# Unit 10's transpose moved from DMA to TensorE, and the unit loads two ahead from unit 10 on

## Chip, cores, metric

One core of one Trainium2 chip; the experiments ran on three chips, and each is compared with before on its own chip. The metric is the device time of one execution in microseconds (us). Times are medians, with the lowest and highest in brackets. The profiled span runs from the first to the last instruction and is about 1.7 us shorter than the time of the same run.

## The reference, cut

```python
# attention with decay: q, k, v (4, 8, 768, 64) float32, lam (8,), blocks along the sequence
intra = (q_b @ k_b.T) * Dmask;  intra = intra @ v_b
inter = (q_b * lam_pow) @ kv_state
out_b = intra + inter
kv_state = lam_block * kv_state + (k_b * rev_pow).T @ v_b
# then x = out, (3072, 512):   a = x @ w_a;  b = x @ w_b;  y = (a * b) @ w_out    # d_ff 1536
```

## The kernel before, the parts that matter

The work is cut into 24 units of 128 tokens, in feed-forward groups of 4, 1, 2, 4, 4, 4, 4 and 1 units. While TensorE does the feed-forward matmuls of one group, the attention pieces of later units are slipped in at numbered slots. In group 2, slots 0 to 11 follow the `a` and `b` matmuls of f = 0 to 11 (the twelve slices of 128 columns of d_ff), and slots 12 to 15 the half rows of the output matmuls `op`. `P` prepares a unit (scaling of k and q on GpSimd, cast of v, and the next loads), `T` transposes on TensorE, `S` makes scores and masks, `V` updates the state, `Q` and `O2` do inter, (scores,) intra. Units 0 to 8 are transposed on TensorE, units 9 to 23 by a DMA transpose that SP issues.

```python
LOOKAHEAD = (3, 2)
DMA_T_FROM = 9
PLAN = { ...
    2: [(0, "V", 6), (1, "T", 7), (1, "P", 8), (4, "T", 8), (4, "P", 9), (6, "S", 7),
        (6, "S", 8), (7, "V", 7), (6, "P", 10), (10, "V", 8),
        (12, "Q", (7, 8, 9, 10)), (12, "P", 11), (13, "V", 9), (14, "P", 12),
        (14, "O2", (9, 10))],
    3: [(3, "S", 11), (3, "S", 12)], ... }

def pump():                       # issue what may be issued, in order, on SP
    while pending:
        kind, c = pending[0]
        if kind in "abo": ...     # weights
        elif c >= used["u"] + LOOKAHEAD[used["u"] > 11]:
            return
        ...

def prep_k(u):
    make_ks(u, "dve" if u < n0 + 2 else "pool")
    make_qs(u, "pool")
    used["u"] = u + 1
    if u >= DMA_T_FROM:
        qkT = qkT_pool.tile(...)
        nc.sync.dma_start_transpose(out=qkT..., in_=U[u]["qk"]...)

def prep_v(u):
    make_vb(u, ...)
    pump()                        # the loads come after this unit's transpose

def piece_T(u):
    tps = ps_bank("tps", [128, 2, HP, 128], BF16)      # one of 7 rotating PSUM banks
    for j in range(2):
        for hp in range(HP):
            nc.tensor.transpose(tps[:, j, hp, :], d["qk"][:, j, 2*hp:2*hp+2, :], ident)
    qkT = qkT_pool.tile(...)
    nc.scalar.copy(qkT, tps)
```

## Time and profile before

| | before |
|---|---|
| time | 234.9 us (234.56 to 235.3) |
| profiled span (that run took 235.62 us) | 233.9 us |
| TensorE busy | 225.5 us, 96% of the span |
| DMA transposes / TensorE transposes `tps` | 15 / 40 |

The kernel is full of TensorE work, so the question is only where TensorE has a hole. The profile's first part, the group of the PSUM copies, and the line of the DMA transposes (count, median us from issue to landing):

```profile
PE 225.5 (96%) x1775; PEld 124.7 (53%) x1775; DVE 118.3 (51%) x204; ACT 91.1 (39%) x172; POOL 50.6 (22%) x65
...
L298 ACT COPY qkT<-tps 128x1024 bf16<-128x1024 bf16 x5 | 5.1, 1012 | 9.9 <-PE tps L296 9.9
```

```profile
qkT<-qk SPq DMA_TRANSPOSE x15, 4.2
```

### The profile page before, as it was taken

What the parts mean: (1) busy time and instruction counts of PE and PEld (TensorE: products, weight loads), DVE (VectorE), ACT (ScalarE), POOL (GpSimd) and SP (SyncE); (2) the same over time, 40 slices, a digit from 0 to 9 for tenths busy, and PEclk for the clock granted to TensorE, in tenths of its full rate; (3) what the DMA queues carried; (4) which work ended last, traced back from release to release, by engine and by line L of the source; (5) the groups of instructions that cost most, each with busy time, mean ns of one, the idle gap of its engine ahead of it and who ended that gap; (6) DMA issues with size and microseconds to landing.
All of it is one profiled execution on the core that took longest, in us unless ns stands there. A gap on an engine that the chain in (4) does not pass through costs nothing.

```text
span 233.9 us, 4520 instructions
## 1 busy us (share of the span) xinstructions
PE 225.5 (96%) x1775; PEld 124.7 (53%) x1775; DVE 118.3 (51%) x204; ACT 91.1 (39%) x172; POOL 50.6 (22%) x65
## 2 busy tenths in 40 slices
PE   7799999999999799999999999999999999999993
PEld 2474444459688454454544454544454544444493
DVE  0896557536579536775235574235583323332050
ACT  3585753066363243342243342333332333332261
POOL 6070000237463333553000543001200000000000
PEclk9999999999999999999999999999999999999999
DMA  4999999999999999998659997229300220000311
GB/s 154 301 286 350 349 366 288 295 191 224 198 229 174 207 220 203 213 193 162 234 198 215 211 178 134 90 90 207 67 3 0 90 92 0 1 0 23 114 45 48
DMA packets 96389, 38.84 MB, mean 166 GB/s; under 512 B 83312, under 2 KB 91888, under 8 KB 96368
## 3 DMA queue, kind: packets, MB, share of 16 engines
q1 hardware_dynamic: 96224, 38.54, 73.3%
q8 instruction: 14, 0.23, 0.4%
q14 instruction: 7, 0.06, 0.1%
q10 hardware_dynamic: 144, 0.00, 0.0%
HBM read 28.32 MB, written 6.29 MB: 148 GB/s over the span
## 4 chain that ended last, share of the span: by engine, by line
PE 90%; DMA 5%; ACT 1%; SPq 1%; issue 0%; DVE 0%
PE a_ps L435 27%; PE b_ps L435 26%; PE op L467 26%; DMA k<-in_k_dram 3%; PE o_ps L352 3%; PE kq L310 2%; DMA qkT<-qk 2%; PE o_ps L342 2%; PE kvd L366 1%; PE tps L296 1%; ACT o_kept L458 1%; SPq L209 1%; PE kq L578 1%; ACT xT L359 0%; PE kv L366 0%; PE tk L542 0%
## 5 line engine op out<-in xcount | busy, mean ns | idle before, releaser
L447 DVE TENSOR_TENSOR ab<-a_sb,b_ps 128x512 bf16<-128x512 bf16 (+2 forms) x96 | 52.5, 553 | 76.7 <-PE b_ps L435 56.7
L435 PE MATMUL a_ps<-xT,wa_sb 128*128 128x512 bf16 (+2 forms) x384 | 77.2, 326 | 0.6 <-ACT xT L359 0.6
L435 PE MATMUL b_ps<-xT,wb_sb 128*128 128x512 bf16 (+2 forms) x384 | 77.3, 326 | 0.0
L442 ACT CAST a_sb<-a_ps 128x512 bf16<-128x512 f32 (+2 forms) x96 | 45.6, 481 | 63.2 <-PE a_ps L435 61.6
L467 PE MATMUL op<-wo_sb,ab 128*128 128x512 bf16 (+2 forms) x312 | 65.6, 363 | 0.0
L435 PEld LDWEIGHTS <-wb_sb 128*128 128x128 bf16 x384 | 34.5, 98 | 28.6
L435 PEld LDWEIGHTS <-wa_sb 128*128 128x128 bf16 x384 | 33.7, 98 | 29.0 <-POOL wa_sb L162 0.6
L467 PEld LDWEIGHTS <-ab 128*128 128x128 bf16 x312 | 28.8, 98 | 29.9
L327 DVE TENSOR_TENSOR m<-kq,lotri 128x512 bf16<-128x512 f32 x47 | 29.4, 684 | 19.3 <-PE kq L310 19.0
L259 POOL TENSOR_TENSOR qk<-kf,lp_k 128x512 bf16<-128x512 f32 x18 | 19.0, 1057 | 76.4 <-DMA kf<-in_k_dram 69.8
L264 POOL TENSOR_TENSOR qk<-qf,lp_q 128x512 bf16<-128x512 f32 x20 | 21.7, 1087 | 23.4 <-DMA qf<-in_q_dram 23.4
L462 ACT COPY o_sb<-op 128x512 f32<-128x512 f32 (+2 forms) x19 | 10.3, 541 | 34.0 <-PE op L467 34.0
L359 ACT CAST xT<-o_ps 128x512 bf16<-128x512 f32 x22 | 12.0, 590 | 19.6 <-PE o_ps L352 19.2
L398 DVE TENSOR_TENSOR st<-kvd,bdiag 128x512 bf16<-128x512 f32 x18 | 12.3, 685 | 4.7 <-PE kvd L366 3.6
L273 DVE CAST vb<-vf 128x512 bf16<-128x512 f32 x17 | 11.3, 667 | 0.0
L298 ACT COPY qkT<-tps 128x1024 bf16<-128x1024 bf16 x5 | 5.1, 1012 | 9.9 <-PE tps L296 9.9
L197 PE MATMUL idle<-idle_sb 128*128 128x128 bf16 (+1 forms) x31 | 7.5, 384 | 1.3 <-DVE idle_sb L192 1.3
L310 PE MATMUL kq<-qkT 64*128 64x128 bf16 x160 | 6.7, 218 | 1.5 <-DMA qkT<-qk 1.5
L352 PE MATMUL o_ps<-m,vb 128*64 128x128 bf16 x192 | 7.9, 222 | 0.0
L273 POOL CAST vb<-vf 128x512 bf16<-128x512 f32 x7 | 4.7, 674 | 13.9 <-DMA vf<-in_v_dram 13.9
L342 PEld LDWEIGHTS <-st 128*128 128x128 bf16 x80 | 5.4, 98 | 2.8
L352 PEld LDWEIGHTS <-vb 128*64 128x64 bf16 x192 | 5.8, 109 | 1.4
(57 smaller groups left out, 87.4 us busy)
## 6 DMA issues: line engine op xcount, KB each, us to landing
vf<-in_v_dram SPq DMA_DIRECT2D x24, 256.0 KB, 5.1
qf<-in_q_dram SPq DMA_DIRECT2D x20, 256.0 KB, 4.5
kf<-in_k_dram SPq DMA_DIRECT2D x20, 256.0 KB, 4.8
out_dram<-o_sb SPq DMA_DIRECT2D x16, 256.0 KB, 2.0
wst<-in_moe_w_a_dram SPq DMA_DIRECT2D x6, 512.0 KB, 8.7
wst<-in_moe_w_b_dram SPq DMA_DIRECT2D x6, 512.0 KB, 8.8
wst<-in_moe_w_out_dram SPq DMA_DIRECT2D x6, 512.0 KB, 8.5
out_dram<-o_kept SPq DMA_DIRECT2D x7, 256.0 KB, 2.5
```

What stands on the lines that cost most here:

```text
L259: eng_of(eng).tensor_mul(qk[:, 1], raw.pop((u, "k")), lp_k[:, u % NB].to_broadcast([128, H, D]))
L264: eng_of(eng).tensor_mul(U[u]["qk"][:, 0], raw.pop((u, "q")), lp_q[:, u % NB].to_broadcast([128, H, D]))
L273: eng_of(eng).tensor_copy(vb, vf)
L310: nc.tensor.matmul(kq[i][:, hp, :], lhsT=d["kT"][p, hp, :], rhs=d["qT"][p, hp, :], start=True, stop=True, skip_group_check=True)
L327: nc.vector.tensor_mul(m, kq[i], lotri_bc)
L352: nc.tensor.matmul(d["o"][p, hp, :], lhsT=d["vb"][:, 2 * hp + i, :], rhs=d["m"](i, hp), start=(first and hp == 0), stop=True, skip_group_c ...
L359: nc.scalar.copy(xT[:, :, col:col + BLK], o_ps)
L398: nc.vector.tensor_mul(st[:].rearrange("p hp i d -> p hp (i d)"), ps[:].rearrange("p hp i d -> p hp (i d)"), bdiag_bc)
L435: nc.tensor.matmul(ps[:, :gt], lhsT=w_sb[:, s, f * 128:(f + 1) * 128], rhs=xT[:, s, :gt], start=(s == 0), stop=(s == KS - 1))
L442: nc.scalar.copy(a_sb[:, :gt], ps[:, :gt])
L447: nc.vector.tensor_mul(ab[:, f, :gt], a_sb[:, :gt], ps[:, :gt])
L467: nc.tensor.matmul(op[:, lo:hi], lhsT=ab[:, f, t * 128:(t + 1) * 128], rhs=wo_sb[:, f, lo:hi], start=(f == 0), stop=(f == FC - 1))
```

## The change

Intent: unit 10's transpose comes too late for its scores, so TensorE does it itself, and the loads are held back one unit from unit 10 on. Unit 9 stays with the DMA.

```diff
-        (6, "S", 8), (7, "V", 7), (6, "P", 10), (10, "V", 8),
+        (6, "S", 8), (7, "V", 7), (6, "P", 10), (9, "T", 10), (10, "V", 8),
-            elif c >= used["u"] + LOOKAHEAD[used["u"] > 11]:
+            elif c >= used["u"] + LOOKAHEAD[used["u"] > 9]:
-        if u >= DMA_T_FROM:
+        if u >= DMA_T_FROM and u != 10:
```

## The prediction

> **What bounds the kernel now.** I read four things in this order: who TensorE waited for, how full TensorE is before and after its longest wait, the instruction around that wait, and the queue that issued the transfer it waited for. All are of the kernel before; its profiled span is 233.9 us against a timed median of 234.9 us.
>
> The list of waits of TensorE (total us, times, longest us), whole for waits over 0.6 us:
>
> ```profile
> PE kq L310 <- DMA qkT<-qk: 1.5, 1, 1.5
> PE idle L197 <- DVE idle_sb L192: 1.3, 1, 1.3
> PE tk L542 <- DVE scratch L531: 0.7, 2, 0.3
> ```
>
> The second and third belong to the first 20 us (warm-up and the packed first group). The only wait of any size in the steady part is the first: the scores `kq` waited once, for a DMA transpose. Busy time of TensorE in stretches (window, length, busy, granted clock, DMA share, GB/s):
>
> ```profile
> 60.00:77.50 17.50, 17.50 (x191) 1.00 1.23 197
> 77.50:79.10 1.60, 0.11 (x6) 1.00 0.98 210
> 79.10:230.40 151.30, 151.24 (x1094) 1.00 0.57 120
> 230.40:233.90 3.50, 0.00 (x0) 1.00 0.22 65
> ```
>
> TensorE has no gap for 17.5 us ahead of that wait and none worth a name for the 151 us after it, at full clock. So the kernel is bound by TensorE, the end moves one for one with TensorE work from 60 us on, and all there is to win here is this one hole. The hole in TensorE's timeline (start, length):
>
> ```profile
> 76.62 0.61 PE L342 MATMUL o_ps<-qkT,st 128*128 128x128 bf16 x8
> 77.16 0.40 PE L310 MATMUL kq<-qkT 64*128 64x128 bf16 x8
> 79.05 0.40 PE L310 MATMUL kq<-qkT 64*128 64x128 bf16 x8 [1.49 <-DMA qkT<-qk]
> ```
>
> This is slot 12 of group 2, `Q (7, 8, 9, 10)`: inter of 7 and 8, scores of 9 (eight matmuls, no wait), scores of 10 (eight, after 1.49 us). So it is unit 10's transpose alone that is late. Why it is late stands in the issue queue of SP and on GpSimd, which makes its source:
>
> ```profile
> 68.12 1.04 POOL L264 TENSOR_TENSOR qk<-qf,lp_q 128x512 bf16<-128x512 f32 x1
> ```
>
> ```profile
> 68.06 2.21 SPq L282 DMA_TRANSPOSE qkT<-qk  x1
> 70.33 0.56 SPq L128 DMA_DIRECT2D qf<-in_q_dram  x1
> 70.94 1.66 SPq L128 DMA_DIRECT2D kf<-in_k_dram  x1
> 72.71 0.83 SPq L128 DMA_DIRECT2D vf<-in_v_dram  x1
> 74.12 1.86 SPq L282 DMA_TRANSPOSE qkT<-qk  x1
> 76.04 0.57 SPq L128 DMA_DIRECT2D qf<-in_q_dram  x1
> 76.67 1.07 SPq L128 DMA_DIRECT2D kf<-in_k_dram  x1
> 77.83 0.86 SPq L128 DMA_DIRECT2D vf<-in_v_dram  x1
> 78.81 3.70 SPq L282 DMA_TRANSPOSE qkT<-qk  x2
> ```
>
> I match these to units by counting: the nine GpSimd pairs up to 92 us are units 6 to 14, and by the program's order the transposes here are 9, 10, then 11 and 12 together, with the loads of unit 12 between 9 and 10 and those of unit 13 between 10 and 11. Unit 10's `qk` was ready at 68.12 + 1.04 = 69.16 us. Its transpose was issued at 74.12, five microseconds later, because SP issues in order and was busy with transpose 9 and the three loads of unit 12. The chain of work that ended last says the rest, and what a transpose on TensorE costs (start, length):
>
> ```profile
> 67.80 0.45 PE tps L296 x8
> ...
> 74.12 4.89 DMA qkT<-qk
> ```
>
> **What the Trainium skill says.** "Perfetto Trace Analysis", section "What "DMA-bound" means", names as a bound of its own the issuing sequencer whose track is solid with DMA slices, this being descriptor generation. The trace agrees for 54.5 to 90 us: SP's slices follow each other within about 0.6 us, a transpose taking 1.86 to 2.21 us. "Advanced Engine Details and Errata", section "X-Bar Transpose (TRN2)", has transposes as fast as ordinary DMAs at 350 to 400 GB/s, for 256 KB an estimated 0.7 us; in this trace they need 3.0 to 5.9 us from issue to landing (median 4.2), so I use the trace. "TensorE: Matmul & The Clock Gate", section "Part 4: PE-mode transpose", gives some 275 ns for one transpose in a kernel, into PSUM, with a copy after it. Here one shows 219 ns, but eight in a row push the next matmul back by only 0.45 us, and the copy on ScalarE takes 1012 ns. Last, "SBUF — State Buffer" says that VectorE and GpSimd share a port pair as an exclusive lock; the `vb` casts at 0.42 to 1.20 us in 60 to 90 us fit that, and I use it only for a margin below.
>
> **The change part by part.**
> 1. Removed: transpose 10 on SP (1.86 us of the queue) and its 4.89 us to landing. The hole of 1.49 us goes if nothing else is late.
> 2. Added on TensorE: eight transposes in slot 9 of group 2. Slot 9 follows the `b` matmuls of f = 9, which end at 73.33 us. The source was ready at 69.16, so there is no wait. Cost +0.45 us, in full on the path, as TensorE has no slack there.
> 3. Added on ScalarE: one copy of 1.01 us, from about 73.97 to 74.98 (0.19 us after the eight end, as for unit 8). It delays the copy `a_sb` of f = 10 from 73.97 to 74.98, f = 11 from 75.09 to about 75.35, then VectorE's product of f = 11 from 76.1 to about 76.8 at its end. That product first matters for the last six `op` matmuls of the row, at about 79 us, and as the release of the PSUM bank that inter of 8 takes. Counting the seven rotating banks through the new order (one more bank taken, by `tps`), unit 8's `o_ps` falls on the bank of `b` of f = 11; TensorE wants it at 77.33 us, the product ends near 76.8. About half a microsecond of slack: beside other work.
> 4. Moved: the threshold of the look-ahead. After unit 9 nothing is loaded, after 10 the loads of 12, after 11 those of 13. SP's order was T9, L12, T10, L13, T11 T12, L14; it becomes T9, L12, T11, L13, T12, L14. Unit 12's loads keep their place at 70.33 (transpose 10 no longer lies ahead of them), transpose 11 takes the place of 10 at 74.12 (its source is ready at 71.70 + 1.04 = 72.74), unit 13's loads stay at about 76. From 80.7 us SP is 1.9 us ahead. TensorE waits for none of these later, so worth on the time: 0.
>
> Scores of 10 are then ready: `qkT` of 10 at 74.98, wanted at 77.16 + 0.45 + 0.40 = 78.0 us. Scores of 9 come 0.45 us later than before, and did not wait then.
> Sum: -1.49 + 0.45 = -1.04 us, so 234.9 - 1.04 = 233.9 us, or -0.44%.
>
> **The rivals.**
> A, the hole moves to VectorE. Masks of 9 and 10 now run one behind the other: from 78.03 us, 4 x 0.64, to about 80.5, then the `vb` cast of 11 (0.42), then the state `st` of 9, done near 81.5 to 81.7. Inter of 10 wants it at 83.0 - 1.04 = 81.95. For it: only 0.3 to 0.5 us of margin, and a cast can take 1.2 us beside GpSimd. Against it: GpSimd has no work from 78.5 to 81.6. It would give back up to 0.6 us: about 234.4.
> B, the DMA wait was hidden anyway or is replaced at once, say by transpose 9 becoming the late one. Then only the 0.45 us would stay: 235.3. Against it: transpose 9 keeps its issue at 68.06, and even with 5.9 us it lands at 74.0, for use at 77.6.
> C, the relief of the queue yields more, because loads and transposes come earlier. For it: the DMA share is about 1.0 up to 121 us. Against it: no TensorE wait after 79.1 us is left to remove (151.24 busy of 151.30). It would make 233.7 at best.
> D, the later loads starve GpSimd (units 12, 13). Against it: the loads hold their times in step 4, and units 11 and 12 are first scored at 92.3 us, with transpose 12 landed by some 86.5. Even 2 us late would show nothing.
>
> **Range and chances.** The sum is of two measured numbers and I trust it to 0.3 us; A may take 0.6 back, and three timed runs of before lie within 234.62 to 235.3. So 233.3 to 234.7. Two per cent is 4.7 us, three times the whole hole, and no rival comes near in either direction: within 2% at 0.98.
>
> **What would show it.** TensorE's wait for `qkT` gone from the list; 48 instead of 40 `tps` matmuls and a sixth copy of 1012 ns; 14 DMA transposes in place of 15; TensorE's busy time in the middle at 100% from 60 us to the end of its work; SP's order as in step 4 with a transpose near 74.1. Step 2 fails if the eight wait for GpSimd; step 3 if a wait of `o_ps` or `kq` on VectorE or ScalarE stands in the list; A if inter (L342) waits for `st`. The prediction is wrong if the time stays at 234.9 or falls under 233.3.

## The result and the profile after

The changed kernel takes 233.68 us (233.63 to 233.75, 5 runs) against 234.9. The ratio is 0.9948, 95% interval 0.9934 to 0.9963, so 0.5% faster. Ratios are the mean time of one kernel's fast runs over that of the other's in the same rounds, so they are not quite the ratio of the medians quoted.

The signs that the prediction named are there: six copies in place of five, 48 `tps` matmuls in place of 40, and 14 DMA transposes in place of 15.

```profile
L298 ACT COPY qkT<-tps 128x1024 bf16<-128x1024 bf16 x6 | 6.1, 1012 | 10.4 <-PE tps L296 10.4
```

```profile
qkT<-qk SPq DMA_TRANSPOSE x14, 4.4
```

Waits of TensorE over 0.5 us after the change (total, times, longest):

```profile
PE idle L197 <- DVE idle_sb L192: 1.3, 1, 1.3
PE tq L542 <- DVE scratch L531: 0.8, 3, 0.4
PE tk L542 <- DVE scratch L531: 0.7, 2, 0.4
PE a_ps L435 <- ACT xT L359: 0.6, 2, 0.5
```

The wait for `qkT` is gone and no new one took its place. TensorE in stretches (window, length, busy, clock, DMA share, GB/s):

```profile
77.50:79.10 1.60, 1.60 (x36) 1.00 1.32 253
79.10:228.40 149.30, 149.30 (x1061) 1.00 0.57 118
```

TensorE's timeline around the old hole:

```profile
73.29 0.61 PE L296 MATMUL tps<-ident,qk 128*128 128x128 bf16 x8
73.73 0.60 PE L435 MATMUL a_ps<-xT,wa_sb 128*128 128x256 bf16 x4
...
77.00 0.61 PE L342 MATMUL o_ps<-qkT,st 128*128 128x128 bf16 x8
77.54 0.62 PE L310 MATMUL kq<-qkT 64*128 64x128 bf16 x16
78.09 0.64 PE L352 MATMUL o_ps<-m,vb 128*64 128x128 bf16 x16
```

The scores of 9 and 10 now run as one batch of 16, from 77.54 to 78.09: 0.55 us. Before, the same 16 went from 77.16 to the start of intra at 79.38 (the timeline has 79.38 for the first matmul of intra): 2.22 us. The difference, 1.67 us, is the real size of the hole. It is 0.18 us more than the 1.49 us that the list of waits shows. The other view that had it was the wait of the weight loads of before:

```profile
79.05 0.23 PEld L310 LDWEIGHTS <-qkT 64*128 64x128 bf16 x8 [1.67 <-DMA qkT<-qk]
```

SP's queue after the change:

```profile
67.94 2.12 SPq L282 DMA_TRANSPOSE qkT<-qk  x1
70.13 1.70 SPq L128 DMA_DIRECT2D qf<-in_q_dram  x1
...
73.66 1.97 SPq L282 DMA_TRANSPOSE qkT<-qk  x1
75.68 0.57 SPq L128 DMA_DIRECT2D qf<-in_q_dram  x1
...
78.26 2.21 SPq L282 DMA_TRANSPOSE qkT<-qk  x1
```

This is T9, L12, T11, L13, T12 (T for a transpose, L for a unit's three loads), and transpose 11 stands where 10 stood.

One number does not fit at first sight. The profiled spans differ by 2.0 us (233.9 and 231.9), the medians by 1.22 us. Two things in these traces lie at the two ends of the program and not in the change's mechanism, so I measure TensorE's part by itself. Call the *TensorE stretch* the time from the first `a_ps` matmul of group 0 to the start of the last copy of results on ScalarE. And call the *store stretch* the time from the first to the last packet of the last three output stores, read from the packet records of the trace. The last column is how long before the first of these packets the last 16 KB instruction fetch (queue q8 of the DMA table) began.

| run | time us | first `a_ps` | TensorE stretch | store stretch | fetch ahead by |
|---|---|---|---|---|---|
| before | 234.9 | 18.57 | 211.81 | 2.14 | 0.50 |
| after | 233.68 | 18.53 | 210.56 | 1.59 | 2.32 |
| e1 | 233.84 | 18.80 | 210.18 | 1.80 | 1.05 |
| e2 | 233.75 | 18.57 | 210.56 | 1.59 | 2.26 |
| e3 | 233.68 | 18.61 | 210.56 | 1.59 | 2.49 |
| e4 | 240.25 | 18.85 | 216.31 | 1.88 | 0.94 |
| e5 | 233.39 | 18.56 | 210.15 | 1.59 | 2.40 |
| e6 | 234.05 | 18.52 | 210.71 | 1.59 | 1.15 |
| e7 | 234.13 | 18.64 | 211.01 | 1.59 | 2.81 |
| e8 | 234.14 | 18.50 | 211.03 | 1.59 | 2.28 |
| e9 | 234.96 | 18.64 | 211.87 | 1.59 | 2.46 |
| e10 | 234.04 | 18.66 | 210.65 | 1.60 | 2.43 |
| e11 | 233.35 | 18.46 | 210.14 | 1.59 | 2.45 |
| e12 | 233.74 | 20.86 | 210.55 | 1.59 | 2.40 |

The stretches are of the one profiled run, the times medians. From before to after, TensorE's stretch shrinks by 1.25 us, about the 1.22 us by which the medians differ. The other 0.7 us of span came from the end of the profiled run of before, which at 235.62 us was slower: its store stretch was 0.55 us longer.

### The profile page after: what moved, and what is told of

The parts are those of the page before. It is cut to its first block, busy times and chain, and to the rows that moved or that the text cites. A ratio compares the mean times of both kernels' runs of the same rounds, so it can differ in the third digit from the quotient of the medians.

```text
span 231.9 us, 4536 instructions
## 1 busy us (share of the span) xinstructions
PE 225.3 (97%) x1783; PEld 125.0 (54%) x1783; DVE 119.0 (51%) x204; ACT 92.0 (40%) x173; POOL 50.4 (22%) x65
## 4 chain that ended last, share of the span: by engine, by line
PE 93%; DMA 3%; ACT 2%; SPq 1%; DVE 0%; issue 0%
PE a_ps L435 27%; PE b_ps L435 27%; PE op L467 27%; DMA k<-in_k_dram 3%; PE o_ps L352 3%; PE kq L310 2%; PE o_ps L342 2%; PE kvd L366 2%; PE tps L296 1%; ACT o_kept L458 1%; SPq L209 1%; PE kq L578 1%; ACT xT L359 0%; PE kv L366 0%; PE tk L542 0%; DVE scratch L531 0%
## 5 line engine op out<-in xcount | busy, mean ns | idle before, releaser
L273 DVE CAST vb<-vf 128x512 bf16<-128x512 f32 x17 | 12.1, 713 | 0.0
L298 ACT COPY qkT<-tps 128x1024 bf16<-128x1024 bf16 x6 | 6.1, 1012 | 10.4 <-PE tps L296 10.4
L197 PE MATMUL idle<-idle_sb 128*128 128x128 bf16 (+1 forms) x31 | 6.9, 363 | 1.3 <-DVE idle_sb L192 1.3
```

Source lines behind the costliest of these rows:

```text
L273: eng_of(eng).tensor_copy(vb, vf)
```

## The experiments

My theory after the result: transpose 10 was late only because of its place in SP's queue, the change removes a hole of 1.67 us and pays 0.45 us of TensorE for it. Rivals: the look-ahead or the load of the DMA engines does it; the transposes are hidden; part of the gain is the end of the program. All kernels gave correct results.

### e1: the look-ahead alone

```diff
 kernel before
-            elif c >= used["u"] + LOOKAHEAD[used["u"] > 11]:
+            elif c >= used["u"] + LOOKAHEAD[used["u"] > 9]:
```

> The kernel before with the look-ahead threshold of the change alone; unit 10 still transposed by DMA. Theory (the wait is transpose 10's place in SP's queue, behind unit 12's loads): the program's order becomes T9, T10, L12, T11, L13, T12, so T10 is issued near 70.3 us instead of 74.1, lands near 75, and the scores of 10 want it at 77.2. TensorE's wait is gone and TensorE has no transposes to pay: 234.9 - 1.67 = about 233.2 us, some 0.45 us under the changed kernel. 15 DMA transposes, 40 tps matmuls. Rival (my prediction's step 4: the look-ahead is worth nothing by itself, the transposes on TensorE are what removes the wait): 234.9 us, wait of 1.5 us still there.

Measured: 233.84 us (233.38 to 233.9; before 234.88 on the same chip). No wait on `qkT` is in the list. SP's queue:

```profile
68.41 4.25 SPq L282 DMA_TRANSPOSE qkT<-qk  x2
72.70 0.58 SPq L128 DMA_DIRECT2D qf<-in_q_dram  x1
```

Transposes 9 and 10 now go out together, ahead of the loads of 12, and TensorE scores both units at once:

```profile
77.43 0.62 PE L310 MATMUL kq<-qkT 64*128 64x128 bf16 x16
```

The mechanism was as the theory had it: TensorE's stretch is 210.18 us, 1.63 us under before and 0.38 us under the changed kernel. The time was not: 233.84 in place of 233.2. In this profile TensorE started 0.27 us later than in the changed kernel's (first `a_ps` 18.80 against 18.53), and the store stretch was 0.21 us longer (1.80 against 1.59). In this profile the two together take the gain back. The rival (the look-ahead is worth nothing by itself) fell.

### e2: unit 10 on TensorE alone

```diff
 changed kernel
-            elif c >= used["u"] + LOOKAHEAD[used["u"] > 9]:
+            elif c >= used["u"] + LOOKAHEAD[used["u"] > 11]:
```

> The changed kernel with the old look-ahead threshold: unit 10 on TensorE, loads three ahead up to unit 11. Theory (with T10 gone from the queue the look-ahead no longer matters): same as the changed kernel, 233.7 us, no wait of TensorE on qkT; SP's order T9, L12, L13, T11, T12. Rival (the look-ahead is needed, since T11 now stands behind the loads of 13): some wait on T11 or T12 at their scores near 91 us, 233.9 to 234.9.

Measured: 233.75 us (233.65 to 234.44), TensorE's stretch 210.56 us as in the changed kernel, no wait on `qkT`. So each half of the change removes the wait by itself, and beside the transposes on TensorE the look-ahead is worth nothing.

### e3: the changed kernel again

> The changed kernel itself, on the same chip as the others. Theory: 233.7 us with a spread under 0.2 us, as there is no wait on a DMA left in the steady part, while the kernel before spreads by 0.7 us. Rival (the small spread was chance, or the gain was): 234.0 to 234.9.

Measured: 233.68 us (233.63 to 233.83), on the chip of e1 and e2, where before spread from 234.29 to 235.58. The gain and the small spread hold.

### e4: transpose 10 still later

```diff
 kernel before
-            elif c >= used["u"] + LOOKAHEAD[used["u"] > 11]:
+            elif c >= used["u"] + (4 if used["u"] == 10 else LOOKAHEAD[used["u"] > 11]):
```

> The kernel before with four units of look-ahead after unit 9, so that the loads of unit 13 too stand ahead of transpose 10. Theory (place in SP's queue): T10 is issued some 2.7 us later (the issue time of unit 13's loads, 76.04 to 78.69), near 76.8, lands near 81.7, and TensorE waits 1.67 + 2.7 = about 4.4 us: 237.6 us. Rival (the landing is slow for another reason, such as the load on the 16 DMA engines, and the place hardly matters): 234.9 to 235.5 us.

Measured: 240.25 us (239.86 to 241.04), ratio 1.0234 (1.0211 to 1.0257). The wait of TensorE, and SP's queue with transposes 10, 11 and 12 behind two units' loads:

```profile
PE kq L310 <- DMA qkT<-qk: 4.6, 1, 4.6
```

```profile
77.81 5.01 SPq L282 DMA_TRANSPOSE qkT<-qk  x3
```

The wait came out as expected (4.56 us listed, 4.4 expected). The rival, a slow landing, can be read from the traces: transpose 10 was issued at 70.81 us in e1, 74.12 in before and 77.81 here, and took 3.96, 4.89 and 4.54 us from issue to landing. The issue moved by 7 us, the time to landing by less than one, so the place in the queue is the cause. The time came out 2.7 us above the expectation. The clock explains half of that. TensorE per microsecond (window, length, busy, granted clock, DMA share, GB/s):

```profile
81.00:82.00 1.00, 0.00 (x0) 1.00 1.00 223
82.00:83.00 1.00, 0.60 (x10) 0.59 1.04 207
83.00:84.00 1.00, 1.00 (x19) 0.50 1.11 203
84.00:85.00 1.00, 1.00 (x4) 0.50 0.70 158
85.00:86.00 1.00, 0.98 (x3) 0.71 1.21 274
```

After the hole TensorE ran at half clock for some three microseconds, and its matmuls take twice the time:

```profile
83.93 2.05 PE L467 MATMUL op<-wo_sb,ab 128*128 128x512 bf16 x5
```

From the scores of 10 to the first `a_ps` of group 3 it took 82.40 to 90.09 = 7.69 us, against 79.05 to 85.31 = 6.26 in before: 1.43 us lost to the clock. The Trainium skill has this in "TensorE: Matmul & The Clock Gate", section "HAM oscillation — how this bites in real kernels": a gap over about 3.4 us throttles TensorE again. The trace agrees: the hole of 4.56 us did it, the hole of 1.49 us in before did not (clock 1.00 throughout). TensorE's stretch grew by 235.16 - 18.85 - 211.81 = 4.50 us in all, that is the longer hole and the clock. The remaining 0.9 us of the 5.4 is mostly the reference's: the profiled run of before, from which its stretch is taken, took 235.62 us, 0.74 over the median of 234.88. Against that very run the profiled span of e4 is longer by 4.5 us (238.4 and 233.9), which is the stretch alone.

### e5 and e11: the look-ahead alone, with the program's end shifted

```diff
 kernel of e1
     warm(13, 512)
+    warm(8, 16)          # 8 tiny matmuls on nothing, where TensorE waits for a load anyway
```

> e1_look_only (look-ahead alone, unit 10 by DMA) with 8 more tiny start-up matmuls (16 columns, in a stretch where TensorE waits anyway), which do no work: TensorE's program then has 3568 rows like the changed kernel, instead of 3552. Theory (e1's TensorE ended 0.1 us before that of the changed kernel, yet its output tail took 4.1 us against 3.75, because a 16 KB instruction fetch on a DMA engine fell into the tail): with the fetch moved earlier the tail takes 3.75 us as in the changed kernel, and the time is 233.84 - 0.35 = 233.5 us or less, at or under the changed kernel's 233.68, nearer 233.3 with e1's saved 0.45 us. Rival (the tail's length is chance or depends on something else): 233.8 us and a tail of 4.1 us.

> The kernel of e5 again, beside the changed kernel on one chip. Theory: 233.4 us, 0.3 us under the changed kernel, spread under 0.2 us. Rival (e5's lead was the chip's): the same as the changed kernel within 0.1 us.

Measured: 233.39 us (233.38 to 233.53), and again 233.35 us (233.28 to 233.47) beside the changed kernel's 233.74 on one chip. Ratios to before 0.9923 (0.9894 to 0.9953) and 0.9911 (0.9865 to 0.9956). TensorE's stretch is as in e1 (210.15 and 210.14), so the eight matmuls change nothing there. The fetch starts 2.40 us ahead of the stores in place of 1.05, and the store stretch is back at 1.59. The issue of the last three stores by SP in before, after, e1 and e5, one fence each:

```profile
229.44 2.12 SPq L463 DMA_DIRECT2D out_dram<-o_sb  x3
```

```profile
228.15 1.57 SPq L463 DMA_DIRECT2D out_dram<-o_sb  x3
```

```profile
228.04 1.77 SPq L463 DMA_DIRECT2D out_dram<-o_sb  x3
```

```profile
227.77 1.56 SPq L463 DMA_DIRECT2D out_dram<-o_sb  x3
```

The two long ones, with e4 (store stretch 1.88 us), are the three profiles in the table in which the fetch, 0.9 to 1.2 us long, was still running when the first store packet went out; in all others it was over. Of the 0.47 us by which the profiled span of e5 is under that of e1, 0.20 us lies after TensorE's end, 0.24 in the start (first `a_ps` 18.80 against 18.56) and 0.03 between. The theory explains the first. The later start of e1 stands already in VectorE's first scaling of q, which waits for the load of q (6.14 us in e1, 5.87 in e5); why that load came later there is open. So about half of e5's lead over e1 in the profiles is not shown to come from the fetch. The lead of e5 and e11 over the changed kernel is another matter: it is the shorter TensorE stretch (by 0.41 and 0.42 us).

### e6: the changed kernel with the end shifted back

```diff
 changed kernel
-        warm(4)              # after each half of the q transposes
+        warm(2)
-            warm(3)          # after two of the k transposes
+            warm(1)
```

> The changed kernel with 8 of its small start-up matmuls on nothing taken out, so that TensorE's program has 3552 rows again, as before the change. Theory (fetch in the tail): the last fetch falls some 1.3 us later, into the output tail, which grows from 3.75 to 4.0 us or more: 233.9 to 234.4 us, with TensorE's end where it was. Rival (no such effect): 233.7 us, tail 3.75.

Measured: 234.05 us (233.67 to 235.33). The profiled run does not show the effect: the fetch moved later (1.15 us ahead in place of 2.32) but ended 0.2 us before the first store, and the store stretch stayed at 1.59. The unprofiled runs are spread wider than any others of the changed kernel with full clock (233.67 to 234.29, and one of 235.33 at a clock of 0.992). The median fits the theory, the profile only half; e2, in which no fetch was moved, spread as wide (233.65 to 234.44). The removed matmuls also stand in the start, so I count this as inconclusive.

### e7: the eight transposes twice

```diff
 changed kernel, piece_T
-                nc.tensor.transpose(tps[:, j, hp, :], ...)
+                for _ in range(2 if u == 10 else 1):
+                    nc.tensor.transpose(tps[:, j, hp, :], ...)
```

> The changed kernel with each of unit 10's eight transposes done twice into the same PSUM place. Theory (the transposes lie in full on TensorE's path, 0.45 us): 233.68 + 0.45 = 234.1 us, and TensorE's end 0.44 us later. Rival (they fill a hole that is there anyway): 233.7 us.

Measured: 234.13 us (234.02 to 236.44, the last at a clock of 0.993). TensorE's stretch grew from 210.56 to 211.01, by 0.45 us:

```profile
73.40 1.06 PE L297 MATMUL tps<-ident,qk 128*128 128x128 bf16 x16
74.29 0.60 PE L436 MATMUL a_ps<-xT,wa_sb 128*128 128x256 bf16 x4
```

Sixteen transposes push the next matmul by 0.89 us, eight by 0.44. The cost is real and lies in full on the path.

### e8: ScalarE's copy twice

```diff
 changed kernel, piece_T
-        nc.scalar.copy(qkT, tps)
+        for _ in range(2 if u == 10 else 1):
+            nc.scalar.copy(qkT, tps)
```

> The changed kernel with the PSUM copy of unit 10 on ScalarE done twice (1.01 us more on ScalarE in slot 9). Prediction's step 3 put about half a microsecond of slack on this side: the product of f = 11 on VectorE ended at 76.60 us in the profile, inter of unit 8 takes its bank at 77.27. Theory: with one more microsecond the slack is used up and TensorE waits some 0.3 to 0.4 us in front of inter of 8 or an op row: 234.0 us. Rival (ScalarE's work there has slack of over a microsecond): 233.7 us with no new wait.

Measured: 234.14 us (234.05 to 234.15). The wait that the prediction's step 3 had feared appears, where it said it would be, at the second half of inter (unit 8), behind VectorE's product:

```profile
PE o_ps L343 <- DVE ab L448: 0.3, 1, 0.3
```

```profile
76.96 0.39 PE L343 MATMUL o_ps<-qkT,st 128*128 128x128 bf16 x4
77.67 0.38 PE L343 MATMUL o_ps<-qkT,st 128*128 128x128 bf16 x4 [0.32 <-DVE ab L448]
```

So one copy fits beside other work and two do not. The listed 0.32 us cost 0.47 us of TensorE's stretch (211.03 against 210.56): again about 0.15 us more than the list says.

### e9: the kernel before with the end shifted

```diff
 kernel before
     warm(13, 512)
+    warm(8, 16)
```

> The kernel before with 8 tiny start-up matmuls more (TensorE's program 3568 rows, as in the changed kernel), nothing else. It parts the gain of the change into the removed wait and the moved instruction fetch. Theory: the wait for transpose 10 stays at about 1.5 us, the output tail (from the first issue of the last three stores to the end of the span) falls to about 3.75 us in place of 4.46 in the profile of before, and the median falls by 0.2 to 0.5 us: 234.4 to 234.7. Rival (the fetch plays no part in the typical run of before): 234.9 us.

Measured: 234.96 us (234.44 to 235.23); before in the same rounds 235.05. The wait is there:

```profile
PE kq L310 <- DMA qkT<-qk: 1.6, 1, 1.6
```

The store stretch is 1.59 us, but the median lies only 0.09 us under before's, less than the 0.2 to 0.5 us that I expected. With 0.8 us of spread, a ratio of 0.9974 (0.9931 to 1.0017) and two runs of before at a lower clock, this can't tell 0.09 from 0.3: what the fetch costs in a typical run of before stays open. e9 and the changed kernel (e12) have TensorE programs of the same length and the same store stretch, and on this one chip e9 takes 1.22 us more (234.96 against 233.74). So the change's 1.22 us are the removed wait and not the end of the program. e9 still spreads by 0.8 us without the fetch in its profiled tail; that the wait makes this spread is likely, but not shown.

### e10: unit 8 by DMA as well

```diff
 kernel of e5
-DMA_T_FROM = 9
+DMA_T_FROM = 8
-... (4, "T", 8), ...
-LOOKAHEAD[used["u"] > 9]
+LOOKAHEAD[used["u"] > 8]
-    warm(8, 16)
+    warm(16, 16)
```

> e5 with unit 8 transposed by DMA as well (DMA from unit 8 on, two units ahead from unit 8 on, 16 tiny start-up matmuls so that TensorE's program keeps 3568 rows). Theory (the queue of SP is full there, so one more transpose pushes the next ones back by its 2 us): SP's order L10, T8, T9, L11, T10, L12; T10 is issued near 71.6 instead of 70.3, lands near 76.4 to 77, and the scores want it at 76.7: a wait of 0 to 0.7 us, some more at unit 8's scores, against 0.45 us saved on TensorE: 233.2 to 234.0, so no clear gain over e5. Rival (there is still room in the queue): 233.39 - 0.45 = 232.95 us with no wait.

Measured: 234.04 us (233.07 to 234.35). Unit 8's scores waited now:

```profile
PE kq L310 <- DMA qkT<-qk: 0.6, 1, 0.6
```

```profile
64.53 3.79 SPq L282 DMA_TRANSPOSE qkT<-qk  x2
...
71.72 2.50 SPq L282 DMA_TRANSPOSE qkT<-qk  x1
```

Transpose 10 was issued at 71.72 as expected and was in time in this run. The saved 0.45 us was more than lost: the stretch is 210.65 us against 210.14 in e11, 0.51 longer. Unit 8's wait cost 0.73: the batch of 16 scores before the next `a_ps` lasted 1.28 us (69.56 to 70.84) in place of 0.55. Another 0.25 is the prediction's rival A: inter of unit 10 took 0.79 us (81.45 to 82.24) in place of 0.54, since the cast of `vb` ahead of the state `st` took 0.92 us in place of 0.42, with GpSimd at work beside it from 79.94 us. The best run (233.07) hints at what the idea could be worth, the median says that it is no gain here.

### e12: the changed kernel beside e11

> The changed kernel beside e11. Theory: 233.68 us, as in the two earlier measurements. Rival: 233.4, as e5.

Measured: 233.74 us (233.68 to 235.93). Four runs lie within 233.68 to 233.78. The other two took 235.73 and 235.93, at a mean clock of 0.993, and the profile caught one of these:

```profile
8.87 0.40 PE L542 MATMUL tq<-ident,scratch 128*128 128x128 bf16 x4 [2.28 <-DVE scratch L531]
```

```profile
9.00:10.00 1.00, 0.80 (x10) 0.74 1.15 320
10.00:11.00 1.00, 1.00 (x11) 0.50 1.14 246
11.00:12.00 1.00, 1.00 (x10) 0.50 1.04 199
12.00:13.00 1.00, 1.00 (x12) 0.56 0.30 66
```

The first loads came 2.2 us later than in the other runs, TensorE stood still for 2.28 us, and the clock then fell to half for three microseconds. Its stretch after the start is 210.55 us, as ever. Before has such runs too (237.7 at 0.991 and 236.98 at 0.993). Since before has them too, I don't put them down to the change, though they blur the ratios of the later calls.

## Why the prediction was right

**The hole goes (step 1).** Right. The term was mis-sized by a tenth: I took 1.49 us from the list of waits of the matmuls, it measured 1.63 to 1.67 (stretch of before against e1; batch times; the weight loads' wait). A wait inside a batch cost more than the list says: 0.18 us here, 0.15 in e8, 0.17 in e10 (0.73 against 0.56). Since the other terms held, this is the whole miss of the sum.

**Eight transposes cost 0.45 us (step 2).** Right: 0.45 by e7, 0.38 to 0.42 by the stretches of the changed kernel against e1, e5 and e11. They started at 73.29 us, predicted 73.33, without a wait.

**ScalarE's copy is hidden (step 3).** Right: it ran at 73.94, predicted 73.97. The product of f = 11 ended at 76.60, predicted 76.8, with inter of 8 wanting it at 77.27. e8 shows that the slack is real and under a microsecond.

**The loads move without effect (step 4).** Right for the change as a whole (e2). But I had stopped at "worth on the time: 0" and did not ask what the look-ahead does with transpose 10 left on the DMA. There it does the whole job at no cost to TensorE (e1, e5), because `prep_k` issues the transpose ahead of the loads that `prep_v` releases. The prediction of the time was not touched by this, the judgement of the change is: its TensorE half is the dearer of two sufficient cures. One reading in the prediction is wrong without effect: between 54.5 and 90 us the transposes held SP for 1.23 to 2.29 us, not 1.86 to 2.21.

**The sum.** -1.04 predicted, -1.22 measured; with the true hole, -1.67 + 0.45 = -1.22.

**The rivals.** A did not come: the state `st` of 9 was done at 81.39 us and inter of 10 wanted it at 81.76, a margin of 0.37 where I had 0.3 to 0.5. It came in e10, where a cast took 0.92 us beside GpSimd. (The prediction cites "SBUF — State Buffer" for such casts without a section; the lock stands there in "SBUF: two separate sides".) B is out, as the wait is gone. C's number (233.7) is what was measured, but not by its mechanism: the look-ahead adds nothing (e2), and after 79.1 us there was no wait to remove; the extra 0.18 us is step 1's. D did not show: TensorE is busy for all of the 149.30 us after 79.1.

## What to carry to other kernels

A late transfer can be a matter of what stands ahead of it in the issuing queue, not of the transfer: before moving the work to the engine that is the bound, try moving the queue. Here that freed TensorE of 0.4 us more than the change; in time it gave 0.3 to 0.4 us more with eight idle matmuls added in the start (e5, e11), and 0.16 less without them (e1). Take the size of a wait from the whole batch before and after it, not from the list of waits alone, and compare engine stretches rather than profiled spans, since the first and last microseconds have accidents of their own. Keep holes in TensorE's work short, because a long one is charged twice: after the 4.56 us of e4 the halved clock cost another 1.43 us.

## What the Trainium skill lacked or had wrong

- "TensorE: Matmul & The Clock Gate", section "Part 4: PE-mode transpose", gives about 275 ns for one transpose. In these runs eight in a row cost TensorE 0.45 us, some 55 ns each, though each record shows 219 ns. The page has this pace for matmuls in a row (55.6 ns at 128 columns), but doesn't say that transposes keep it.
- The same page, section "HAM oscillation — how this bites in real kernels", puts the limit of a gap at about 3.4 us. The hole of 4.56 us in e4 agrees, and the 1.67 us in before left the clock at 1.00. But in e12 the clock fell to 0.50 at about 9.5 us, after a hole of 2.28 us and four transposes, 2.9 us after the last ordinary matmul. Whether transposes count as work for the clock was not tested here; either way the gap was under 3.4 us.
- "Advanced Engine Details and Errata", section "X-Bar Transpose (TRN2)", gives only a bandwidth for a transpose's speed. What counted here is how long transfers hold the issuing queue, a transpose most of all: 1.2 to 2.8 us (median 2.0) in before, where a load of q took as little as 0.56 us.
- "Runtime: NRT & Kernel Launch", section "Instruction fetch mechanics", has the refills of 16 KiB and calls their cost mostly hidden. It lacks what one does to a transfer beside it: here they are 16 KB each on queue q8, the last one 0.9 to 1.2 us long, and where it ran into the last stores (before, e1, e4) these took 2.14, 1.80 and 1.88 us in place of 1.59. That they belong to TensorE's program is inferred from e5 and e9, where 16 rows more there (8 matmuls and their weight loads) started the last one 1.4 and 2.0 us earlier against the stores.
